# Squares of twelve weight blocks taken as products on TensorE instead of passes on ScalarE, with new booked lengths in the planner and one more block asked early

## The chip, the cores and the metric

The kernel runs on one core of a Trainium2 chip. The metric is the device time of one execution in microseconds (us). Engines are named as in the profile: PE is TensorE (its weight loads stand apart as PEld), DVE is VectorE, ACT is ScalarE, POOL is GpSimd, SP is SyncE, which only asks for DMA transfers here.

## The reference

Three layers follow each other: a two-sided attention, a feed-forward layer with squared ReLU, and a layer of eight experts of which each token uses one.

```python
def _attn_ref(x, state):            # x 8,8,512,64   state 8,8,32,64
    scores = scale * x @ state^T;  a = softmax(scores);   xread = a @ state
    scores2 = scale * state @ x^T; a2 = softmax(scores2); sread = a2 @ x
    return concatenate([xread, sread], axis=2)
def _moe_ref(x, w_in, w_out):       # 4608 x 512, 512 x 2048, 2048 x 512
    r = np.maximum(x @ w_in, 0.0)
    return (r * r) @ w_out
def _moe2_ref(x, expert_emb, tau, w1, w2):
    expert_idx = argmax(logits)     # logits: cosine of x and expert_emb, over tau
    out[mask] = gate_w * (np.maximum(x[mask] @ w1[e], 0.0) @ w2[e])
```

The two weights w_in and w_out come as float64; the rest is float32.

## The kernel before

PE multiplies in 16-bit halves: a float32 operand is scaled by a power of two and split into a high and a low half, and three products stand for one. The scale of each 256-column block of w_in comes from the largest sum of squares of its columns, the scale of w_out from the sum of all its squares. So every weight block passes ScalarE and VectorE several times before PE can use it, and this work fills the first 100 us.

The 8 MB of each float64 weight come in 16 blocks of 1 MB, in the order of `BLOCKS`: two blocks of w_in ("i"), two of w_out ("o"), and so on: blocks 0, 1, 4, 5, 8, 9, 12, 13 are w_in's i0 to i7, blocks 2, 3, 6, 7, 10, 11, 14, 15 w_out's o0 to o7. `weights()` asks for them one after the other on SP's queue; from block `AHEAD` on only after the two DMA transposes of the first attention (L553) are asked. For each block, `to_f32` (L900)
- converts the upper parts of the 1024 numbers on ACT into a "top", one of two tiles that alternate (rec_128 and rec_129 in the order rows; L915),
- widens the top into the block's float32 place, on ACT (L922) or DVE (L925), whichever has less booked,
- adds the lower bits on DVE (L928), and lets the scale be worked out: `wi_scale` (L941) squares a w_in block on ACT (L947), sums the squares down the columns with four PE products against a tile of ones (L955), takes the largest on DVE (L961); `wo_square` (L1000) squares and sums a w_out block in one ACT pass (L1006).

With the scale (swi) known, the state of the first attention times the block (L668) is split on ACT and DVE into sw (L677, L317), and the up-projection of the first 256 tokens (unit 0) can run on PE (L1395 to L1397); its ReLU is ACT L1348, its square ACT L1352, and its down-projection is done in float32 on PE (L1458), two weight blocks at a time. The weight blocks themselves are split on ACT (L993, L1054) and DVE (L317).

The order of the instructions on every engine is written by a planner (class `Plan`) when the program is built: threads yield an engine and a booked length (`act(n)`, `dve(n)`, `pe(k, n)`), and the one that can start first goes next, with a priority for ties. The booked lengths decide the order only; each engine then works its list strictly in that order. Further names: ps_t and ps_u are pools of two PSUM banks each (tiles "t" and "u"), `stage`, `he`, `g`, `wo_t` are places where raw blocks land, and rid is a small table (34.5 KB) asked behind block 9; SP's next request, of rec_d, waits for a POOL copy of it (L1872).

Of the kernel before, what the change touches and what calls it, by code (L numbers as in the profile page):

```python
# [10 lines left out]
F32 = mybir.dt.float32  # L11
# [38 lines left out]
LOADER = 9  # L50
AHEAD = 5
PRIO_A0 = 0.8
# [193 lines left out]
def moe_kernel(  # L246
# [79 lines left out]
    def splits(pieces, n):  # L326

        at, times = plan.now(), []
        for hi, lo, src, scale in pieces:
            yield act(n) + (at,)  # L330
            nc.scalar.activation(out=hi, in_=src, func=AF.Copy, scale=scale)
            times.append(plan.now())
        for (hi, lo, src, scale), t in zip(pieces, times):
            yield dve(n) + (t,)
            split_lo(lo, src, scale, hi)
# [115 lines left out]
    def attention(b):  # L451
# [8 lines left out]
        for i in range(2):  # L460
            q = slice(2 * i, 2 * i + 2)
            yield act(1024)
            nc.scalar.activation(out=xh.bitcast(BF16)[:, q], in_=xf[:, q], func=AF.Square, accum_out=ss[:, i:i + 1])
        yield act(256)
        nc.scalar.activation(out=xl.bitcast(BF16)[:, :, :64], in_=stt, func=AF.Square, accum_out=ss[:, 2:3])
# [98 lines left out]
    def first_attention():  # L564

        yield ev("st", 0)
        stt = st_t.pop(0)
        yield xhl_slots
        xh, xl = halves_tile()
        ss = small.tile([128, 3], F32, name="ss")  # L570
        yield act(256)
# [39 lines left out]
    def first_scale(ss, stt):  # L611
# [6 lines left out]
        for i in range(2):  # L618
            yield pjk_slots
            jk = att.tile([128, 2, 512], BF16, name="pjk")  # L620
            yield act(1024)
            nc.scalar.activation(out=jk, in_=xf[:, 2 * i:2 * i + 2], func=AF.Square, accum_out=ss[:, i:i + 1])
            pjk_slots.release()
# [126 lines left out]
    def state_side(b, pairs, scl):  # L750
# [21 lines left out]
        for C, p in enumerate(ps):  # L772
# [4 lines left out]
                            op1=ALU.mult)  # L777
            yield act(700)
            nc.scalar.activation(out=e2[:, C, :], in_=p, func=AF.Exp, scale=scl, bias=mt[:, C:C + 1],
# [115 lines left out]
    def to_f32(n, dst, squares, squared):  # L895
# [4 lines left out]
        if not W64:  # L900
            w = raw.bitcast(F32)
            plan.add(squares(w), plan.cur[1])
            for m in over:
# [3 lines left out]
        else:  # L907
# [5 lines left out]
            top = tops[k_t % 2]  # L913
            yield act(1024)
            nc.scalar.activation(out=top.bitcast(F16), in_=raw.bitcast(BF16)[:, :, 2], func=AF.Copy)  # L915
            at = plan.now()
            for m in over:
                yield ev("read", m)
            plan.cur[2] = max(at, plan.now())
# [12 lines left out]
        plan.add(freed(n, slots, squared), plan.cur[1])  # L932

    def freed(n, slots, squared):
# [5 lines left out]

    def wi_scale(q, w):  # L941
        at = plan.now()
        yield pjk_slots
        plan.cur[2] = max(at, plan.now())
        sq = att.tile([128, 4, BW], BF16, name="pjk")
        yield act(1024)
        nc.scalar.activation(out=sq, in_=w.rearrange("p (k f) -> p k f", k=4), func=AF.Square)  # L947
        ev("wisq", q).set()
# [3 lines left out]
        p, k_h = ps_u.tile([128, 512], F32, name="u"), u_slots.last()  # L952
        yield pe(4, BW)
# [10 lines left out]
        if q % 2:  # L964
# [5 lines left out]
            v = w  # L970
            V.tensor_scalar(out=v, in0=v, scalar1=FLOOR, scalar2=None, op0=ALU.max)
            pow2(swi[:, qs], iswi[:, qs], v, 204)
# [7 lines left out]
    def wi_block(n, q):  # L980
        yield ev("raw", n)
        yield from to_f32(n, wi32[q].rearrange("p k f -> p (k f)"), lambda a: wi_scale(q, a), ev("wisq", q))
        ev("wi32", q).set()
        plan.add(wi_split(q), PRIO_SPLIT)
# [14 lines left out]

    def wo_square(q, w):  # L1000
# [4 lines left out]
        yield act(1024)  # L1005
        nc.scalar.activation(out=jk, in_=w, func=AF.Square, accum_out=woacc[:, q:q + 1])  # L1006
        pjk_slots.release()
        ev("wosq", q).set()

    def wo_block(n, q):  # L1010
        yield ev("raw", n)
        yield from to_f32(n, wo32[q].rearrange("p k d -> p (k d)"), lambda a: wo_square(q, a), ev("wosq", q))
        ev("f32", q).set()

    def weights():
# [13 lines left out]
        V.tensor_reduce(out=ismin[:, 0:1], in_=iswi, axis=X, op=ALU.max)  # L1029
        yield from tensor_scale(woacc, smin[:, 1:2], ismin[:, 1:2])  # L1030
        yield tiny(3)
# [27 lines left out]

    def tensor_scale(acc, s, inv):  # L1060

# [10 lines left out]
        yield tiny(4)  # L1072
        V.tensor_scalar(out=w, in0=p[:, 0:1], scalar1=FLOOR, scalar2=None, op0=ALU.max)
        t_slots.release()
# [3 lines left out]
    def experts():  # L1078
# [46 lines left out]
        def scale():  # L1125
            for i in range(2 * NE):
# [3 lines left out]
                for n in range(2 * i, 2 * i + 2):  # L1130
                    yield ev("stage", n)
                    for a in range(2):
                        yield pjk_slots
                        jk = att.tile([128, 1024], BF16, name="pjk")
                        col = 2 * (n % 2) + a
                        yield act(1024)
                        nc.scalar.activation(out=jk, in_=halves[n].bitcast(F32)[:, a * 1024:a * 1024 + 1024],
# [73 lines left out]
    def route_tile(i, ps, k_h, rc, st):  # L1211
# [3 lines left out]
        if i < 2 * F32U:  # L1215
            yield ev("wo scale")
        yield act(600)
        nc.scalar.activation(out=rc[:, 0:512].bitcast(BF16), in_=ps, func=AF.Square, accum_out=st["f2"][:, j:j + 1],
# [719 lines left out]
```

## Time and profile before

| | us |
|---|---|
| three runs | 1081.05, 1079.14, 1084.92; median 1081.05 |
| profiled execution, its own time | 1085.53 |
| its span in the trace | 1083.7 |
| busy in the span: PE | 1034.8 (95%) |
| DVE | 669.9 (62%) |
| ACT | 600.3 (55%) |
| POOL | 122.9 (11%) |

The profiled execution takes 1.8 us more than its span and lies 0.4% above the median of the runs. Busy shares are means over stages: in the first 110 us the weights and the first attention are prepared, from there to about 610 us the rest of attention and the first two layers run, then the experts.

### The profile page before, as it was taken

How to read it: one execution, taken by the hardware profiler on the slowest of the kernel's cores; microseconds unless marked ns; L12 is line 12 of the kernel's file. 1: busy time of each engine (PE TensorE's matmuls, PEld its weight loads, DVE VectorE, ACT ScalarE, POOL GpSimd, SP SyncE). 2: the span in 40 equal slices, each digit the busy share in tenths (PEclk: the TensorE clock that was granted, in tenths of full speed). 3: DMA queues.
4: the chain of work that ended last, by engine and by line, in shares of the span. 5: the costliest groups of instructions: out<-in, count | busy, mean ns of one | idle time of the engine just before them, and what ended most of it. 6: DMA issues, size and time to landing. Idle time of an engine off the chain costs nothing. (4 is left out here: it accounts for less than half of the span.)

```text
span 1083.7 us, 26223 instructions
## 1 busy us (share of the span) xinstructions
PE 1034.8 (95%) x10553; PEld 667.1 (62%) x10553; DVE 669.9 (62%) x1818; ACT 600.3 (55%) x1003; POOL 122.9 (11%) x149
## 2 busy tenths in 40 slices
PE   5789999899999999999999999999999999999998
PEld 4345465455565555656565666677676766767674
DVE  6779888778798877788887873465222222322222
ACT  6999898878887878879888783211111110101010
POOL 0000002002001001020010010321112111112111
PEclk9999999999999999999999999999999999999999
DMA  8843566755836655756766778834895767684792
GB/s 272 321 172 106 143 200 159 247 164 171 237 116 167 212 139 183 214 137 204 211 210 219 252 212 295 224 81 137 309 237 159 212 173 216 198 249 150 168 295 87
DMA packets 161599, 212.91 MB, mean 196 GB/s; under 512 B 112257, under 2 KB 115201, under 8 KB 156098
## 3 DMA queue, kind: packets, MB, share of 16 engines
q1 hardware_dynamic: 152722, 184.04, 58.1%
q0 software_dynamic: 8320, 27.08, 7.7%
q8 instruction: 84, 1.38, 0.5%
q14 instruction: 41, 0.34, 0.1%
q10 hardware_dynamic: 432, 0.08, 0.0%
HBM read 259.10 MB, written 51.68 MB: 287 GB/s over the span
## 5 line engine op out<-in xcount | busy, mean ns | idle before, releaser
L1745 ACT ACTIVATE r<-u 128x512 f32<-128x512 f32 x70 | 41.8, 597 | 323.3 <-PE u L1791 294.0
L1481 PE MATMUL d<-wo_t,g 128*128 128x512 f16 x512 | 194.1, 379 | 1.8 <-DVE g L1367 1.7
L1479 PE MATMUL d<-wo_t,g 128*128 128x512 f16 x512 | 194.0, 379 | 1.5 <-DVE g L1365 0.6
L1480 PE MATMUL d<-wo_t,g 128*128 128x512 f16 x512 | 194.0, 379 | 0.0
L1395 PE MATMUL u<-aT,sw 128*128 128x256 f16 x512 | 141.1, 276 | 7.7 <-ACT sw L677 4.3
L1397 PE MATMUL u<-aT,sw 128*128 128x256 f16 x512 | 140.8, 275 | 1.3 <-DVE sw L317 0.7
L1396 PE MATMUL u<-aT,sw 128*128 128x256 f16 x512 | 140.9, 275 | 0.5 <-issue 0.4
L1748 DVE CAST hh<-r 128x512 f16<-128x512 f32 x70 | 30.0, 429 | 137.3 <-ACT r L1745 135.8
L1348 ACT ACTIVATE r<-u,cg 128x512 f32<-128x512 f32 x128 | 87.5, 683 | 46.8 <-PE u L1397 22.8
L1759 DVE TENSOR_SCALAR o<-d,rec,wo_t 128x512 f32<-128x512 f32 x35 | 28.3, 809 | 107.6 <-PE d L1814 107.5
L1367 DVE TENSOR_TENSOR g<-r,g 128x512 f16<-128x512 f32 x128 | 87.7, 687 | 9.8 <-ACT r L1362 7.8
L1321 POOL DMA_INDIRECT rec_d<-rec,pi x34 | 37.6, 1105 | 494.0 <-DVE mt L774 91.2
L1814 PEld LDWEIGHTS <-hh 128*128 128x128 f16 (+1 forms) x688 | 54.6, 102 | 57.1 <-issue 0.4
L1481 PEld LDWEIGHTS <-g 128*128 128x128 f16 x512 | 50.0, 98 | 63.6 <-DVE g L1367 3.7
L1362 ACT ACTIVATE r<-r 128x512 f32<-128x512 f32 x128 | 80.2, 628 | 1.5
L1479 PEld LDWEIGHTS <-g 128*128 128x128 f16 x512 | 50.3, 98 | 49.2 <-DVE g L1365 1.1
L1480 PEld LDWEIGHTS <-g 128*128 128x128 f16 x512 | 50.1, 98 | 47.7 <-issue 0.9
L1789 PE MATMUL u<-xes,stage 128*128 128x128 f16 x448 | 76.1, 219 | 0.4 <-issue 0.4
L1790 PE MATMUL u<-xes,stage 128*128 128x128 f16 x448 | 76.1, 219 | 0.0
L1791 PE MATMUL u<-xes,stage 128*128 128x128 f16 x448 | 76.1, 219 | 0.0
L1395 PEld LDWEIGHTS <-sw 128*128 128x128 f16 x512 | 51.4, 100 | 33.0 <-issue 16.7
L1789 PE MATMUL u<-xes,xx 128*128 128x128 f16 x416 | 70.5, 219 | 0.0
(331 smaller groups left out, 2564.8 us busy)
## 6 DMA issues: line engine op xcount, KB each, us to landing
w_d<-he SPq DMA_DIRECT2D x128, 256.0 KB
g<-w_d SPq DMA_DIRECT2D x16, 2048.0 KB
wo_t<-w_d SPq DMA_DIRECT2D x16, 2048.0 KB
stage<-w_d SPq DMA_DIRECT2D x14, 2048.0 KB
he<-w_d SPq DMA_DIRECT2D x14, 2048.0 KB
xx<-w_d SPq DMA_DIRECT2D x13, 2048.0 KB
sw<-w_d SPq DMA_DIRECT2D x13, 2048.0 KB
stage<-in_w_dram SPq DMA_DIRECT2D x20, 1024.0 KB
```

The source lines that it names most:

```text
L1348: nc.scalar.activation(out=r, in_=ps, func=AF.Relu, scale=cg[:, g:g + 1] if u >= F32U else cgq[:, c:c + 1])
L1362: nc.scalar.activation(out=r, in_=r, func=AF.Square)
L1367: V.tensor_tensor(out=gl, in0=r, in1=gh, op=ALU.subtract)
L1395: mm(o, lhsT=hl[:, i, 0, fs], rhs=aT[:, i, :], start=i == 0, stop=False)
L1396: mm(o, lhsT=hl[:, i, 0, fs], rhs=aT[:, 2 + i, :], start=False, stop=False)
L1397: mm(o, lhsT=hl[:, i, 1, fs], rhs=aT[:, i, :], start=False, stop=i == 1)
L1479: mm(ps, lhsT=g_h[:, f, ts], rhs=w[:, 0, :], start=f == 0, stop=False)
L1480: mm(ps, lhsT=g_h[:, f, ts], rhs=w[:, 1, :], start=False, stop=False)
L1481: mm(ps, lhsT=g_l[:, f, ts], rhs=w[:, 0, :], start=False, stop=f == KF - 1)
L1789: mm(p[:, j, xs], lhsT=w[:, 0, k, fs], rhs=xe[:, k, xs], start=k == 0, stop=False)
L1790: mm(p[:, j, xs], lhsT=w[:, 0, k, fs], rhs=xe[:, 4 + k, xs], start=False, stop=False)
L1791: mm(p[:, j, xs], lhsT=w[:, 1, k, fs], rhs=xe[:, k, xs], start=False, stop=k == 3)
```

## The change

For blocks 4 to 15 (`GRAM`) the squares are no longer passes on ACT. Eight PE products of the block's top with itself (128 by 128 each, every one with its own weights) are summed in a bank of ps_t; the diagonal holds the sums of squares. For w_in a DVE multiplication with the identity (128 x 256) leaves the diagonal, and one PE product with the ones in place of four spreads the sums; for w_out DVE multiplies (128 x 128) and sums (128 x 128). Since the tops lack the lower bits, the sums get a margin of 1.14 and 1.13. A top is now free again only when its products are done. The planner's `act(...)` bookings change: passes with a sum are booked at 1260 instead of 1024, the strided conversion at 1130, splits 100 longer, and so on; this alters no instruction, only the order. `AHEAD` is 6 instead of 5. The bookings and the new threads also move instructions on all engines.

```diff
-AHEAD = 5
+AHEAD = 6
+GRAM = tuple(range(4, 16))
@@ splits
-            yield act(n) + (at,)
+            yield act(n + 100) + (at,)
@@ attention (and alike at the other passes with a sum)
-            yield act(1024)
+            yield act(1260)
@@ to_f32
-            yield act(1024)
+            yield act(1130)
             nc.scalar.activation(out=top.bitcast(F16), in_=raw.bitcast(BF16)[:, :, 2], func=AF.Copy)
+            gram = n in GRAM
+            if gram:
+                plan.add(squares(top, True), plan.cur[1])
...
-            top_slots.release(k_t)
...
-            plan.add(squares(dst), plan.cur[1])
+            if gram:
+                plan.add(topped(k_t, squared), plan.cur[1])
+            else:
+                top_slots.release(k_t)
+                plan.add(squares(dst, False), plan.cur[1])
@@ wi_scale
+        if gram:
+            yield t_slots
+            p = ps_t.tile([128, 512], F32, name="t")[:, 0:BW].rearrange("p (c m) -> p c m", c=2)
+            yield pe(8, 140)
+            for c in range(2):
+                for k in range(4):
+                    mm(p[:, c], lhsT=w[:, k, c], rhs=w[:, k, c], start=k == 0, stop=k == 3)
+            ev("wisum", q).set()
...
+            yield dve(BW)
+            V.tensor_tensor(out=sq.rearrange("p k (c m) -> p (k c) m", c=2), in0=p,
+                            in1=ident16.unsqueeze(1).to_broadcast([128, 2, 128]), op=ALU.mult)
+            t_slots.release()
...
-        for k in range(4):
-            mm(p[:, 0:BW], lhsT=oneb, rhs=sq[:, k, :], start=k == 0, stop=k == 3)
+        for k in range(ks):
+            mm(p[:, 0:BW], lhsT=oneb, rhs=sq[:, k, :], start=k == 0, stop=k == ks - 1)
@@ wo_square
+        if gram:
+            yield t_slots
+            p = ps_t.tile([128, 512], F32, name="t")[:, 0:128]
+            yield pe(8, 140)
+            for c in range(8):
+                mm(p, lhsT=w[:, 128 * c:128 * c + 128], rhs=w[:, 128 * c:128 * c + 128], start=c == 0, stop=c == 7)
+            yield dve(128)
+            V.tensor_tensor(out=p, in0=p, in1=ident16, op=ALU.mult)
+            yield dve(128)
+            V.tensor_reduce(out=woacc[:, q:q + 1], in_=p, axis=X, op=ALU.add)
```

Three places in the order of the instructions matter below. The first is PE just ahead of the first up-projection. Before, the last products with the ones for i1 (L955) stand there, and the up-projection follows:

```order
L955 LDWEIGHTS oneb
L955 MATMUL u<-pjk,oneb 128x256
L1395 LDWEIGHTS sw
L1395 MATMUL u<-aT,sw 128x256
L1396 LDWEIGHTS sw
L1396 MATMUL u<-aT,sw 128x256
```

In the changed kernel the same place (L962 are products of tops, L1442 and L1443 the up-projection) reads:

```order
L962 LDWEIGHTS rec_129
L962 MATMUL t<-rec_129 128x128
L1442 LDWEIGHTS sw
L1442 MATMUL u<-aT,sw 128x256
L1443 LDWEIGHTS sw
L1443 MATMUL u<-aT,sw 128x256
```

Sixteen products, eight of block 4 (rec_128) and eight of block 5 (rec_129), now stand between the ones of i1 and the first up-projection.

The second place is ACT from the first split of sw on. Before (L677 sw, L993 split of a w_in block, L1348 and L1352 ReLU and square of unit 0):

```order
L677 ACTIVATE sw<-S_250,swi 128x512
L993 ACTIVATE wi<-wi,swi 128x1024
L677 ACTIVATE sw<-S_251,swi 128x512
L915 ACTIVATE rec_129<-g 128x1024
L922 CAST wi<-rec_129 128x1024
L947 ACTIVATE pjk<-wi 128x1024
L915 ACTIVATE rec_128<-he 128x1024
L1348 ACTIVATE r<-u,cgq 128x512
L947 ACTIVATE pjk<-wi 128x1024
L1352 ACTIVATE g<-r 128x2x2x128
L922 CAST wo_t<-rec_128 128x1024
```

In the changed kernel (L678 sw, L1023 split, L916 conversion, L926 widening, L1052 square of a w_out block, L1395 and L1399 ReLU and square):

```order
L678 ACTIVATE sw<-S_248,swi 128x512
L1023 ACTIVATE wi<-wi,swi 128x1024
L678 ACTIVATE sw<-S_249,swi 128x512
L916 ACTIVATE rec_129<-g 128x1024
L916 ACTIVATE rec_128<-he 128x1024
L926 CAST wi<-rec_129 128x1024
L1052 ACTIVATE pjk,woacc<-wo_t 128x1024
L1395 ACTIVATE r<-u,cgq 128x512
L926 CAST wo_t<-rec_128 128x1024
L1399 ACTIVATE g<-r 128x2x2x128
L916 ACTIVATE rec_129<-wo_t 128x1024
L1023 ACTIVATE wi<-wi,swi 128x1024
```

The two squares L947 have left this stretch, a square of a w_out block that stood ahead of it has come in, and conversions of later blocks have moved up.

The third place is SP's queue at the start. Before (L339 is every plain load, L553 the transposes):

```order
L339 DMA stage<-in_w_out_dram 128x2x2048 x2
L339 DMA g<-in_w_in_dram 128x4x1024
L553 DMA_TRANSPOSE aT<-xx 128x8x128 x2
L339 DMA g<-in_w_in_dram 128x4x1024
L339 DMA he<-in_w_out_dram 128x2x2048
L339 DMA wo_t<-in_w_out_dram 128x2x2048
```

In the changed kernel:

```order
L340 DMA stage<-in_w_out_dram 128x2x2048 x2
L340 DMA g<-in_w_in_dram 128x4x1024 x2
L554 DMA_TRANSPOSE aT<-xx 128x8x128 x2
L340 DMA he<-in_w_out_dram 128x2x2048
L340 DMA wo_t<-in_w_out_dram 128x2x2048
```

Block 5 (the second g) has moved ahead of the two transposes; the order of the requests behind it, down to the tables, rec_d, block 10 and the second x, is as before.

## Rows read from the trace of the kernel before

**Rows 1.** Windows by stage: length, busy time of each engine, granted PE clock, DMA share, GB/s

```profile
27.00:54.00 27.00, 21.13 (x141) 10.46 (x142) 21.06 (x44) 24.40 (x33) 2.20 (x5) 0.96 0.85 321
54.00:81.00 27.00, 24.07 (x123) 12.66 (x124) 19.76 (x49) 25.31 (x38) 1.42 (x2) 0.91 0.47 170
```

**Rows 2.** Timeline of PE: start, length, what [idle before, released by]

```profile
28.96 0.40 PE L1395 MATMUL u<-aT,sw 128*128 128x256 f16 x1 [3.85 <-ACT sw L677]
...
36.43 0.42 PE L1396 MATMUL u<-aT,sw 128*128 128x256 f16 x1
36.64 0.42 PE L1397 MATMUL u<-aT,sw 128*128 128x256 f16 x1
...
39.08 0.27 PE L1397 MATMUL u<-aT,sw 128*128 128x256 f16 x1
39.19 7.03 PE L1458 MATMUL d<-wo_t,g 128*128 128x512 f32 x16
...
51.38 0.61 PE L955 MATMUL u<-pjk,oneb 128*128 128x256 bf16 x4 [2.54 <-ACT r L1348]
...
64.00 0.39 PE L471 MATMUL t<-ss,one 128*128 128x3 f32 x2 [1.92 <-ACT xx L465]
...
65.52 1.01 PE L955 MATMUL u<-pjk,oneb 128*128 128x256 bf16 x4 [1.01 <-ACT pjk L947]
...
91.48 3.60 PE L1458 MATMUL d<-wo_t,g 128*128 128x512 f32 x8
```

**Rows 3.** Windows of 2 us, columns as in rows 1

```profile
52.00:54.00 2.00, 2.00 (x33) 0.78 (x34) 1.98 (x3) 2.00 (x4) 0.00 (x0) 0.50 1.01 406
54.00:56.00 2.00, 2.00 (x4) 0.94 (x5) 0.78 (x1) 2.00 (x5) 0.00 (x0) 0.69 1.05 387
...
66.00:68.00 2.00, 2.00 (x11) 1.37 (x10) 1.74 (x10) 2.00 (x3) 0.00 (x0) 0.50 0.65 264
68.00:70.00 2.00, 2.00 (x26) 1.01 (x24) 1.53 (x2) 1.36 (x3) 0.00 (x0) 0.78 0.00 0
```

**Rows 4.** Timeline of ACT, columns as in rows 2

```profile
30.41 1.12 ACT L915 ACTIVATE rec<-g 128x1024 f16<-128x1024 bf16 x1
31.57 1.04 ACT L922 CAST wi<-rec 128x1024 f32<-128x1024 bf16 x1
32.52 1.05 ACT L947 ACTIVATE pjk<-wi 128x1024 bf16<-128x1024 f32 x1
33.48 1.10 ACT L915 ACTIVATE rec<-he 128x1024 f16<-128x1024 bf16 x1
34.48 0.67 ACT L1348 ACTIVATE r<-u,cgq 128x512 f32<-128x512 f32 x1
...
43.69 1.06 ACT L1006 ACTIVATE pjk<-wo_t 128x1024 bf16<-128x1024 f32 x1
...
44.73 1.16 ACT L915 ACTIVATE rec<-stage 128x1024 f16<-128x1024 bf16 x1
...
48.69 1.12 ACT L915 ACTIVATE rec<-he 128x1024 f16<-128x1024 bf16 x1 [1.75 <-DMA he<-in_w_out_dram]
```

**Rows 5.** Timelines of SP and POOL and windows: block 9, tables, block 10

```profile
43.52 0.41 SPq L339 DMA_DIRECT2D he<-in_w_out_dram  x1
...
41.88 1.19 POOL L1872 COPY rec<-rid 128x1 int32<-128x1 int32 x1 [40.10 <-DMA rid<-in_rowid_dram]
...
22.00:24.00 2.00, 1.11 (x16) 0.33 (x17) 2.00 (x4) 2.00 (x4) 0.00 (x0) 1.00 0.02 4
```

**Rows 6.** Prices: a DVE pass over 256 numbers in PSUM, two 128-column products

```profile
38.73 0.42 DVE L961 TENSOR_REDUCE wv<-u 128x1 f32<-128x256 f32 x1 [2.24 <-PE u L955]
...
700.05 0.22 PE L1789 MATMUL u<-xes,xx 128*128 128x128 f16 x1
700.10 0.22 PE L1790 MATMUL u<-xes,xx 128*128 128x128 f16 x1
```

**Rows 7.** PE's waits from 100 us to the end: us in total, times, longest

```profile
PE t L471 <- ACT xx L465: 3.0, 4, 1.2
```

More of the change, by code (lines that the diff above doesn't have):

```diff
@@ L461, in attention @@
             q = slice(2 * i, 2 * i + 2)
-            yield act(1024)
+            yield act(1260)
             nc.scalar.activation(out=xh.bitcast(BF16)[:, q], in_=xf[:, q], func=AF.Square, accum_out=ss[:, i:i + 1])
-        yield act(256)
+        yield act(490)
         nc.scalar.activation(out=xl.bitcast(BF16)[:, :, :64], in_=stt, func=AF.Square, accum_out=ss[:, 2:3])
@@ L570, in first_attention @@
         ss = small.tile([128, 3], F32, name="ss")
-        yield act(256)
+        yield act(490)
         nc.scalar.activation(out=xl.bitcast(BF16)[:, :, :64], in_=stt, func=AF.Square, accum_out=ss[:, 2:3])
@@ L620, in first_scale @@
             jk = att.tile([128, 2, 512], BF16, name="pjk")
-            yield act(1024)
+            yield act(1260)
             nc.scalar.activation(out=jk, in_=xf[:, 2 * i:2 * i + 2], func=AF.Square, accum_out=ss[:, i:i + 1])
@@ L777, in state_side @@
                             op1=ALU.mult)
-            yield act(700)
+            yield act(920)
             nc.scalar.activation(out=e2[:, C, :], in_=p, func=AF.Exp, scale=scl, bias=mt[:, C:C + 1],
@@ L901, in to_f32 @@
             w = raw.bitcast(F32)
-            plan.add(squares(w), plan.cur[1])
+            plan.add(squares(w, False), plan.cur[1])
             for m in over:
@@ L913, in to_f32 @@
             top = tops[k_t % 2]
-            yield act(1024)
+            yield act(1130)
             nc.scalar.activation(out=top.bitcast(F16), in_=raw.bitcast(BF16)[:, :, 2], func=AF.Copy)
-            at = plan.now()
+            converted = plan.now()
+            gram = n in GRAM
+            if gram:
+                plan.add(squares(top, True), plan.cur[1])
             for m in over:
                 yield ev("read", m)
-            plan.cur[2] = max(at, plan.now())
+            plan.cur[2] = max(converted, plan.now())
             if plan.load("act") < plan.load("dve"):
@@ L929, in to_f32, with topped @@
                                    op0=ALU.logical_shift_right, op1=ALU.bitwise_or)
-            plan.add(squares(dst), plan.cur[1])
+            if gram:
[3 more added lines that the diff above has]
+                plan.add(squares(dst, False), plan.cur[1])
             squared = ev("raw", n)
         plan.add(freed(n, slots, squared), plan.cur[1])
+    def topped(k_t, squared):
+        yield squared
+        top_slots.release(k_t)
     def freed(n, slots, squared):
@@ L939, in moe_kernel, with wi_scale @@
     wv = {}
-    def wi_scale(q, w):
+    def wi_scale(q, w, gram):
+        if gram:
+            at = plan.now()
+            yield t_slots
+            plan.cur[2] = max(at, plan.now())
+            p = ps_t.tile([128, 512], F32, name="t")[:, 0:BW].rearrange("p (c m) -> p c m", c=2)
+            w = w.rearrange("p (k c m) -> p k c m", k=4, c=2)
+            yield pe(8, 140)
[3 more added lines that the diff above has]
+            ev("wisum", q).set()
         at = plan.now()
@@ L944, in wi_scale @@
         plan.cur[2] = max(at, plan.now())
-        sq = att.tile([128, 4, BW], BF16, name="pjk")
-        yield act(1024)
-        nc.scalar.activation(out=sq, in_=w.rearrange("p (k f) -> p k f", k=4), func=AF.Square)
+        ks = 1 if gram else 4
+        sq = att.tile([128, 4, BW], BF16, name="pjk")[:, :ks]
+        if gram:
[3 more added lines that the diff above has]
+            t_slots.release()
+        else:
+            yield act(1024)
+            nc.scalar.activation(out=sq, in_=w.rearrange("p (k f) -> p k f", k=4), func=AF.Square)
+            ev("wisum", q).set()
         ev("wisq", q).set()
@@ L952, in wi_scale @@
         p, k_h = ps_u.tile([128, 512], F32, name="u"), u_slots.last()
-        yield pe(4, BW)
-        for k in range(4):
-            mm(p[:, 0:BW], lhsT=oneb, rhs=sq[:, k, :], start=k == 0, stop=k == 3)
+        yield pe(ks, BW)
+        for k in range(ks):
+            mm(p[:, 0:BW], lhsT=oneb, rhs=sq[:, k, :], start=k == 0, stop=k == ks - 1)
         pjk_slots.release()
@@ L970, in wi_scale @@
             v = w
-            V.tensor_scalar(out=v, in0=v, scalar1=FLOOR, scalar2=None, op0=ALU.max)
+            V.tensor_scalar(out=v, in0=v, scalar1=1.14, scalar2=FLOOR, op0=ALU.mult, op1=ALU.max)
             pow2(swi[:, qs], iswi[:, qs], v, 204)
@@ L981, in wi_block @@
         yield ev("raw", n)
-        yield from to_f32(n, wi32[q].rearrange("p k f -> p (k f)"), lambda a: wi_scale(q, a), ev("wisq", q))
+        yield from to_f32(n, wi32[q].rearrange("p k f -> p (k f)"), lambda *a: wi_scale(q, *a), ev("wisum", q))
         ev("wi32", q).set()
@@ L998, in moe_kernel, with wo_square @@
     woacc = small.tile([128, NB], F32, name="woacc", bufs=1)
-    def wo_square(q, w):
+    def wo_square(q, w, gram):
+        if gram:
+            at = plan.now()
+            yield t_slots
+            plan.cur[2] = max(at, plan.now())
+            p = ps_t.tile([128, 512], F32, name="t")[:, 0:128]
+            yield pe(8, 140)
+            for c in range(8):
+                mm(p, lhsT=w[:, 128 * c:128 * c + 128], rhs=w[:, 128 * c:128 * c + 128], start=c == 0, stop=c == 7)
+            ev("wosum", q).set()
+            yield dve(128)
+            V.tensor_tensor(out=p, in0=p, in1=ident16, op=ALU.mult)
+            yield dve(128)
+            V.tensor_reduce(out=woacc[:, q:q + 1], in_=p, axis=X, op=ALU.add)
+            t_slots.release()
+            ev("wosq", q).set()
+            return
         at = plan.now()
@@ L1004, in wo_square @@
         jk = att.tile([128, 1024], BF16, name="pjk")
-        yield act(1024)
+        yield act(1260)
         nc.scalar.activation(out=jk, in_=w, func=AF.Square, accum_out=woacc[:, q:q + 1])
         pjk_slots.release()
+        ev("wosum", q).set()
         ev("wosq", q).set()
@@ L1011, in wo_block @@
         yield ev("raw", n)
-        yield from to_f32(n, wo32[q].rearrange("p k d -> p (k d)"), lambda a: wo_square(q, a), ev("wosq", q))
+        yield from to_f32(n, wo32[q].rearrange("p k d -> p (k d)"), lambda *a: wo_square(q, *a), ev("wosum", q))
         ev("f32", q).set()
@@ L1029, in weights @@
         V.tensor_reduce(out=ismin[:, 0:1], in_=iswi, axis=X, op=ALU.max)
-        yield from tensor_scale(woacc, smin[:, 1:2], ismin[:, 1:2])
+        yield from tensor_scale(woacc, smin[:, 1:2], ismin[:, 1:2], 1.13)
         yield tiny(3)
@@ L1058, in wo_split, with tensor_scale @@
         ev("wo", q).set()
-    def tensor_scale(acc, s, inv):
+    def tensor_scale(acc, s, inv, margin=1.0):
         v = small.tile([128, 1], F32, name="fv")
@@ L1072, in tensor_scale @@
         yield tiny(4)
-        V.tensor_scalar(out=w, in0=p[:, 0:1], scalar1=FLOOR, scalar2=None, op0=ALU.max)
+        V.tensor_scalar(out=w, in0=p[:, 0:1], scalar1=margin, scalar2=FLOOR, op0=ALU.mult, op1=ALU.max)
         t_slots.release()
@@ L1135, in scale @@
                         col = 2 * (n % 2) + a
-                        yield act(1024)
+                        yield act(1260)
                         nc.scalar.activation(out=jk, in_=halves[n].bitcast(F32)[:, a * 1024:a * 1024 + 1024],
@@ L1216, in route_tile @@
             yield ev("wo scale")
-        yield act(600)
+        yield act(740)
         nc.scalar.activation(out=rc[:, 0:512].bitcast(BF16), in_=ps, func=AF.Square, accum_out=st["f2"][:, j:j + 1],
```

## The prediction

> **What bounds the kernel now.** I read the windows by stage first, then PE's timeline, then that of ACT, and last the queues. PE is busy for 1034.8 of 1083.7 us, so outside the first 100 us the time is almost wholly PE's own work, which the change leaves alone apart from its products of tops. What can be won are PE's waits and its slow stretches. In the windows of 27 to 54 and 54 to 81 us [rows 1] PE stands still for 5.9 and 2.9 us, while ACT is busy for 24.4 and 25.3 of 27: ACT is what the start hangs on. PE's timeline [rows 2] names the waits behind the first up-projection: 2.54 us until 51.38 (a bank of ps_u that ACT's ReLU frees late), 1.92 until 64.00 (the attention's squares on ACT) and 1.01 until 65.52 (a weight block's square on ACT): 5.5 us.
>
> Two of these waits are followed by a stretch at the lower clock. The granted clock is 0.50 and 0.69 in the two windows from 52 and 0.50 and 0.78 in the two from 66 [rows 3]; with 2.4 GHz as 1.00, PE lost 1.0 + 0.6 + 1.0 + 0.4 = 3.1 us of full speed there. (At the start the spacing of 256-column products says the same: 0.21 us at 36.43, the level of 1.2 GHz, 0.11 us at 39.08, that of 2.4 GHz [rows 2].) So between 39.19, when the float32 down-projection of unit 0 begins, and its end at 91.48 + 3.60 = 95.08 [rows 2], 5.5 + 3.1 = **8.6 us** are not work.
>
> **The change, part by part.** *ACT.* Six squares L947 go, at 0.96 us from start to start (32.52 to 33.48), and six L1006, at 1.04 (43.69 to 44.73) [rows 4]: 12.0 us. By the order three more widenings (10 in place of 7) stand on ACT at 0.95 each (31.57 to 32.52): 2.9 back, so ACT has 9.1 us less to do before the weights are ready. That covers the 8.6, if the time comes out at the places where PE waits. It does by the order: the attention's squares come nine places earlier in ACT's list and its x is late only by the load (below), and no pass of a weight block stands between a product of tops and its sum.
>
> *DVE.* Six multiplications over 256 numbers in PSUM at about the 0.42 of L961 [rows 6], six pairs over 128 at no more than that each, less three widenings: some 3 to 5 us more. DVE is busy for 21.1 and 19.8 of 27 us [rows 1], so its idle time hides it; without that cover it would come on top.
>
> *PE.* 96 products of 128 columns at 0.055 us (two of them start 700.05 and 700.10, at a neighbouring spacing of 0.05 to 0.06, each with a weight load of its own [rows 6]) and 18 fewer products with the ones at 0.11. For blocks 8 to 15, which fall behind the start of the down-projection, that is 64 x 0.055 - 12 x 0.11 = **+2.2 us**, all on the path, since PE sets the end there.
>
> *The first up-projection.* It now stands behind the products of block 5, which need that block's conversion. The passes ahead of this conversion (sw, a split, sw) are the same, so it runs from 30.4 to 31.4 as now [rows 4], and eight products at the lower clock (twice 0.055) end at 32.3: 3.3 us later than 28.96. But the first ReLU comes no later: behind that conversion ACT has a conversion (1.00), a widening (0.95) and a square (1.04), and reaches the ReLU at 34.4, against 34.48 now [rows 4]. So PE's delay meets ACT's own pace. The start of the down-projection then slips by something between nothing and the whole 3.3; 16 products at the lower clock (1.8) less six with the ones (1.3) are 0.5 more work until there, and I take **+1.1**, nearer the lower end, because the ReLUs set the pace.
>
> *The early block.* The DMA engines stand idle from 22 to 24 us (share 0.02 [rows 5]), between the loads asked before the transposes and those after. With block 5 asked ahead, its 1 MB (2.6 us at the 390 to 405 GB/s of the windows from 52 [rows 3]) fills the gap. Blocks 6 to 9 are still asked behind the transposes; these come about 2 us later, because in ACT's order the copy that they turn now stands behind the square of i1. Four blocks then take 10.5 us from about 27, and the table rid, asked behind them, lands near 39.9, against 41.88 now, when POOL's copy starts [rows 5]. Block 10 waits for that copy and would be asked at 41.5 in place of 43.52 [rows 5]; now its conversion starts at 48.69 [rows 4], and x, one load behind, is there 2.6 us later, at 51.3: it would land near 49.3. These 2 us matter, since ACT now stands ready for x at about 47, directly behind block 10's conversion; now ACT waits 1.75 us for block 10 [rows 4]. The Trainium skill (DMA: Bandwidth & Descriptors, Queues, rings and completion order) says that each DMA engine consumes the descriptors of a queue in the order of its ring. By that rule rid moves up with the bulk ahead of it and the sum is the one taken here; were rid's landing tied to nothing ahead of it, the first rival's would hold. The trace agrees so far: five loads of 2.6 us from about 25 end near 39, and the copy that waits for rid starts at 41.88 [rows 5].
>
> From x at 49.3 ACT has, by its order, twenty passes to the fifth square of unit 0; between the 0.67 of a ReLU and the 1.12 of a conversion [rows 4], and each 0.1 shorter from start to start, I take 0.8 as their mean: 65.3. PE comes to the fifth down-projection from 40.3 with four of them (14.2, from 7.03 and 3.60 [rows 2]), 48 products of the up-projection (5.3), 56 of tops (3.1) and some 3 us of small work, at about 65.9. ACT is ahead of PE by about half a microsecond: enough, but no more. So the waits of 2.54, 1.92 and 1.01 should go, and with them the slow stretches.
>
> *The bookings.* They change no pass, only where PE's list has the product that follows the attention's squares (L471). The old booking was 2 x 0.95 + 0.31 = 2.26 us by the formula of `act`, the measured passes take about 2.5, the new booking is 2.80. Behind 100 us PE waits 3.0 us in four places for these squares [rows 7]. Four times 0.54 is the most that this can give back, 2.2; nothing is the least, and a worse order elsewhere could cost as much; I take **1.0**.
>
> **Sum:** -8.6 + 2.2 + 1.1 - 1.0 = -6.3 us. Against the profiled execution's own 1085.53 (span 1083.7 and 1.8 around it) that is 1079.2. The runs' median is 4.5 us lower, and a saving in the start is as large there: 1081.05 - 6.3 = **1075** us.
>
> **The rivals.** *The waits come back elsewhere.* For it: ACT's lead on PE is some 0.6 us, and x is a load that no engine can hasten. If rid lands no earlier, x comes at 51.3, the third pair of the down-projection slips by 2 us, and a wait of that size was followed by 1.4 to 1.6 us at the lower clock in both places [rows 3]. Of the 6.3 then 2.7 stay: 1078. Against it: the gap in the DMA's work at 22 us is plain and block 5 fits into it.
>
> *Slower.* PE works its list strictly in order, and the sixteen products of blocks 8 and 9 stand ahead of the third chunk's up-projection. If block 9's conversion on ACT comes d later than PE wants it, PE waits d, the chunk's ReLU comes later, and the slow stretch follows (1.6). If the old waits also remain because ACT is filled by its widenings, the time is 2.2 + 1.1 + 1.6 + d above now, which passes 5.4 from d = 0.5 on; with d = 2 it is 1088. Against it: that conversion stands twelve passes of about 0.8 behind the first ReLU at 34.4, so near 45, and PE, busy with 7.03 us of float32 work [rows 2] from 40.3, asks for it at 47.3.
>
> *More.* The lead holds, the bookings give their 2.2 and the down-projection starts no later: -8.6 + 2.2 - 2.2 = -8.6, or 1072.5.
>
> **How the numbers follow.** About 0.5% (5.4 us) is what a measurement of this kernel can tell from no change. The forecast has 0.58, with a range of its own from 1072.5 to 1079 (the 3.3 and the two bounds of the bookings); 0.42 of it lies beyond 5.4 and 0.16 within. The waits that come back have 0.25 (within), more has 0.10 (faster), slower 0.07. That makes faster 0.52, within 0.5% 0.41, slower 0.07. The range from 1070 to 1082 takes in the first three and leaves out the slower case and the far ends.
>
> **What would show it.** Right: the last float32 down-projection of unit 0 ends near 90 instead of 95; the first up-projection starts near 32.3 and the first ReLU still near 34.4; no wait of PE over 1 us and no window below 0.9 of the clock between 42 and 90; ACT busy about 9 us less in all; POOL's copy of rid starts near 40. Wrong: waits of PE for a conversion (ACT rec) ahead of products of tops, or for x's squares near 50; a clock of 0.50 in a window behind 42; a down-projection that starts behind 42; or a start that is 6 us shorter with as much more idle time of PE between 110 and 650, where the order is new as well.

## The result: 0.7% slower

The changed kernel takes 1088.54 us (median of 8 runs, 1086.62 to 1093.91), the kernel before 1081.09 (8 runs): ratio 1.0072, 95% interval 1.005 to 1.0094. The forecast was 1075, and its range ended at 1082. The profiled execution took 1086.81 us (span 1084.9). ACT is busy for 591.3 us in place of 600.3, PE for 1034.9 in place of 1034.8.

The start went much as forecast. Windows by stage of the changed kernel, columns as in [rows 1]:

```profile
27.00:54.00 27.00, 22.00 (x189) 13.72 (x190) 23.08 (x50) 23.79 (x30) 1.36 (x5) 1.00 0.85 309
54.00:81.00 27.00, 26.31 (x181) 14.91 (x180) 24.81 (x61) 24.83 (x34) 0.61 (x2) 1.00 0.43 158
```

PE's timeline of the changed kernel, as in [rows 2]:

```profile
27.68 1.04 PE L962 MATMUL t<-rec 128*128 128x128 bf16 x8 [3.67 <-ACT rec L916]
31.97 1.03 PE L962 MATMUL t<-rec 128*128 128x128 bf16 x8 [3.25 <-ACT rec L916]
...
87.43 3.60 PE L1505 MATMUL d<-wo_t,g 128*128 128x512 f32 x8
```

From 54 to 81 us PE now stands still for 0.7 us in place of 2.9, and the clock is 1.00 in place of 0.91. The last float32 down-projection of unit 0 ends at 91.03 in place of 95.08 [rows 2]. The products of tops wait 3.67 and 3.25 us for their conversions, ahead of the first up-projection. So there is a lead of 4 us at 91, and a loss of 7 at the end. Where it goes is best seen in a second pair of traces, taken when both kernels ran once more (medians 1078.87 and 1072.82 us; below). The two are of different chips, on which the kernel before takes 1072.70 and 1072.61 us. In them, PE's busy time in three windows and then 676 to 700, of the changed kernel:

```profile
100.00:300.00 200.00, 195.24 (x1768) 114.42 (x1768) 164.96 (x432) 166.76 (x291) 10.98 (x16) 1.00 0.62 171
300.00:500.00 200.00, 198.44 (x1744) 117.81 (x1742) 165.70 (x463) 168.28 (x294) 18.95 (x24) 1.00 0.68 186
500.00:676.00 176.00, 174.41 (x1323) 107.90 (x1320) 130.53 (x410) 131.72 (x217) 20.32 (x24) 1.00 0.75 230
676.00:700.00 24.00, 15.01 (x164) 12.72 (x163) 3.55 (x10) 2.57 (x5) 2.00 (x3) 0.82 1.09 214
```

and the same windows of the kernel before:

```profile
100.00:300.00 200.00, 192.21 (x1711) 113.11 (x1710) 162.51 (x422) 168.91 (x296) 12.38 (x16) 1.00 0.65 185
300.00:500.00 200.00, 196.89 (x1755) 116.47 (x1754) 164.23 (x466) 165.52 (x291) 17.35 (x24) 1.00 0.59 167
500.00:676.00 176.00, 173.72 (x1336) 108.28 (x1335) 131.51 (x389) 132.82 (x216) 10.19 (x15) 1.00 0.75 231
676.00:700.00 24.00, 23.27 (x247) 15.68 (x245) 11.17 (x48) 5.86 (x11) 10.32 (x11) 1.00 0.94 234
```

Up to 676 the new order is even the denser one: 568.1 us of PE work against 562.8, 5.3 more. Then PE does 15.01 us of work in 24, at a mean clock of 0.82, where the kernel before does 23.27 at 1.00. PE's timeline there, first the kernel before (its last float16 down-projection), then the changed kernel:

```profile
689.76 0.38 PE L1481 MATMUL d<-wo_t,g 128*128 128x512 f16 x1
```

```profile
679.27 0.38 PE L1528 MATMUL d<-wo_t,g 128*128 128x512 f16 x1
686.30 0.27 PE L1836 MATMUL u<-xes,stage 128*128 128x128 f16 x1 [6.64 <-DMA xes<-rec]
...
696.66 0.22 PE L1836 MATMUL u<-xes,xx 128*128 128x128 f16 x1 [2.34 <-DMA xes<-rec]
...
1048.82 0.20 PE L1836 MATMUL u<-xes,g 128*128 128x64 f16 x1 [2.69 <-issue]
```

```profile
686.00:690.00 4.00, 3.70 (x36) 3.73 (x37) 0.00 (x0) 0.00 (x0) 0.00 (x0) 0.50 1.11 309
```

The changed kernel reaches the end of the second layer 10.5 us sooner (679.27 against 689.76; the layer ends near 690, not at the 610 that the section on the profile gives). Then it waits 6.64 and 2.34 us for xes, the transposed tokens of the first two expert tiles, and behind the first wait it works at a granted clock of 0.50 until about 691 (the last row). It loses the lead and 5 us more. Over 676 to 700, 8.3 us of this are more idle time of PE. The later wait of 2.69 (behind nothing that the profile names) is hardly part of it, because the kernel before has one of 2.1 too. The first pair of traces shows waits of 5.89 and 1.50 us for xes at the same place.

Why xes is late stands on SP's queue. The changed kernel: stores of the experts' split weights (w_d), three loads of 2 MB each (L1742), the first transposed load (L1782):

```profile
653.54 1.00 SPq L340 DMA_DIRECT2D w_d<-he  x2
656.86 0.37 SPq L1742 DMA_DIRECT2D stage<-w_d  x1
658.91 0.34 SPq L1742 DMA_DIRECT2D he<-w_d  x1
660.76 0.34 SPq L1742 DMA_DIRECT2D xx<-w_d  x1
673.40 1.36 SPq L1782 DMA_TRANSPOSE xes<-rec  x1
```

The kernel before, in the other trace of this pair:

```profile
647.30 3.85 SPq L339 DMA_DIRECT2D w_d<-he  x4
653.31 0.36 SPq L1695 DMA_DIRECT2D stage<-w_d  x1
655.36 0.34 SPq L1695 DMA_DIRECT2D he<-w_d  x1
663.64 0.35 SPq L1695 DMA_DIRECT2D xx<-w_d  x1
679.87 1.25 SPq L1735 DMA_TRANSPOSE xes<-rec  x1
```

In the kernel before, the three loads are asked 37, 35 and 26 us ahead of the end of the second layer (690.14); in the changed kernel 23, 21 and 19 us (679.65). They wait for the experts' chain, in which ACT and DVE scale and split eight experts' weights that go to memory and come back. By the new order its last store is asked 3.4 us later (654.54 against 651.15), although PE is 10.5 us ahead. The first transposed load of the changed kernel is asked at 673.40, and its tokens reach PE at 686.30, 12.9 us later. Of that, 3.9 us pass until its first packet moves, at 677.3, and the last packet of the three loads ends at 678.3. The other 9.0 us the transposed load itself is under way. Windows of the changed kernel:

```profile
671.00:676.00 5.00, 5.00 (x25) 2.25 (x23) 1.90 (x10) 0.36 (x1) 2.99 (x3) 1.00 0.97 393
676.00:681.00 5.00, 3.65 (x17) 1.47 (x15) 0.47 (x4) 0.69 (x2) 2.00 (x3) 1.00 1.17 189
```

The DMA engines move 393 GB/s until 676. Over the next 5 us they are as busy (share 1.17) but move 189: POOL's gathers and the transposes, xes among them, now run at the same time in small packets. No run takes these two apart.

### The profile page after: what moved, and what is told of

Read it like the earlier page. It is cut to its first block, busy times and chain, and to the rows that moved or that the text cites. A ratio compares the mean times of both kernels' runs of the same rounds, so it can differ in the third digit from the quotient of the medians.

```text
span 1084.9 us, 26367 instructions
## 1 busy us (share of the span) xinstructions
PE 1034.9 (95%) x10631; PEld 673.0 (62%) x10631; DVE 671.9 (62%) x1835; ACT 591.3 (54%) x986; POOL 123.4 (11%) x149
## 5 line engine op out<-in xcount | busy, mean ns | idle before, releaser
L1442 PE MATMUL u<-aT,sw 128*128 128x256 f16 x512 | 140.5, 274 | 4.3 <-ACT r L1395 3.5
L1443 PE MATMUL u<-aT,sw 128*128 128x256 f16 x512 | 140.2, 274 | 0.0
L1395 ACT ACTIVATE r<-u,cg 128x512 f32<-128x512 f32 x128 | 87.3, 683 | 54.8 <-PE u L1444 40.9
L1836 PE MATMUL u<-xes,stage 128*128 128x128 f16 x448 | 77.8, 222 | 5.9 <-DMA xes<-rec 5.9
L1837 PE MATMUL u<-xes,stage 128*128 128x128 f16 x448 | 77.8, 222 | 0.0
L1838 PE MATMUL u<-xes,stage 128*128 128x128 f16 x448 | 77.7, 222 | 0.0
L1836 PE MATMUL u<-xes,xx 128*128 128x128 f16 x416 | 70.5, 219 | 1.5 <-DMA xes<-rec 1.5
L1838 PE MATMUL u<-xes,xx 128*128 128x128 f16 x416 | 70.4, 219 | 0.0
```

Of the source, the lines that this page charges most:

```text
L1395: nc.scalar.activation(out=r, in_=ps, func=AF.Relu, scale=cg[:, g:g + 1] if u >= F32U else cgq[:, c:c + 1])
L1442: mm(o, lhsT=hl[:, i, 0, fs], rhs=aT[:, i, :], start=i == 0, stop=False)
L1443: mm(o, lhsT=hl[:, i, 0, fs], rhs=aT[:, 2 + i, :], start=False, stop=False)
L1836: mm(p[:, j, xs], lhsT=w[:, 0, k, fs], rhs=xe[:, k, xs], start=k == 0, stop=False)
L1837: mm(p[:, j, xs], lhsT=w[:, 0, k, fs], rhs=xe[:, 4 + k, xs], start=False, stop=False)
L1838: mm(p[:, j, xs], lhsT=w[:, 1, k, fs], rhs=xe[:, k, xs], start=False, stop=k == 3)
```

## The experiments

They ran on three chips, on each of which the kernel before takes 1072 to 1073 us (1081 in the first result); each ratio is to runs of the kernel before on the same chip. The first four texts use these theories: A, PE's lead is lost at the change to the experts, because the first xes stands behind late loads; B, the gather or the weights themselves are late; C, the products of tops cost the time.

**The order of two requests.** The third load is held until the first xes is asked (after and, as a control, before):

```diff
                         yield ev("moe1") if name == "w2" else ev("cum", NXT - 1)
+                        if name == "w1":
+                            yield ev("xe", 0)
```

> The changed kernel, with the load of the second expert tile's first weight (2 MB into xx) asked only behind the first turned tile (xes) instead of ahead of it; up to 660 us its order is the same. Theory A (the start is shorter, but PE comes to the experts 9 us earlier and stands there, because the first xes queues behind 2 MB that were asked late): the wait of 5.9 us at 685 and the slow clock behind it go, the time falls by 6 to 9 us against the changed kernel, to a ratio of 0.997 to 1.001 against the kernel before. Rival B (PE waits there for the gather or the weights themselves): the wait stays within 1.5 us of 5.9 and the ratio near 1.007. Rival C (the products or the early part cost the time): no change, 1.007.

Measured 1.0001 (0.9982 to 1.002): as A expected, outside B and C. SP's queue and PE's timeline of this run:

```profile
660.07 0.37 SPq L1744 DMA_DIRECT2D stage<-w_d  x1
662.13 0.34 SPq L1744 DMA_DIRECT2D he<-w_d  x1
675.07 1.27 SPq L1784 DMA_TRANSPOSE xes<-rec  x1
...
682.42 0.35 SPq L1744 DMA_DIRECT2D xx<-w_d  x1
```

```profile
679.30 0.22 PE L1838 MATMUL u<-xes,stage 128*128 128x128 f16 x1 [1.70 <-DMA xes<-rec]
...
692.30 0.22 PE L1838 MATMUL u<-xes,xx 128*128 128x128 f16 x1 [2.09 <-DMA xx<-w_d]
```

With one load fewer ahead of it, xes reaches PE 4.2 us after it is asked, not 12.9. The held load is now itself late (2.09 at 692.30), so part of the gain goes back. The Trainium skill (DMA: Bandwidth & Descriptors, Queues, rings and completion order) says that each DMA engine takes the descriptors of a queue in the order of its ring. By that rule a small transfer waits for the bulk ahead of it, and the trace agrees in part: with the third load held, the first packet of xes moves 2.2 us after its request (677.3) in place of 3.9. The larger part of the 8.7 us is behind that: from its first packet to PE it takes 2.0 us in place of 9.0, now that most of the gathers are through before it.

> The same edit in the kernel before, as a control. A: PE does not wait for xes there, so within 2 us of the kernel before (0.998 to 1.002). If the edit itself is good or bad for another reason, it shows here too.

Measured 1.0041 (1.0022 to 1.006), outside what A expected: in the kernel before the same two lines make PE wait 2.3 us for the held load. So they are no gain in themselves; they help only where xes is in the way.

**The bookings alone.** The changed kernel with the old `act(...)` numbers, and the kernel before with the new ones:

```diff
-            yield act(1260)
+            yield act(1024)
...
-            yield act(n + 100) + (at,)
+            yield act(n) + (at,)
```

> The changed kernel with the old bookings of ACT's passes: products of tops and the early block alone. In its order the first xes stands ahead of the 2 MB load by itself. A: the start ends about 4 us earlier than in the kernel before, no wait above 2 us at the start of the experts, ratio 0.992 to 0.998. C (the products cost the time): 1.005 or more.

Measured 1.0101 (1.0075 to 1.0127). PE's waits in the old-bookings run:

```profile
96.96 0.27 PE L1442 MATMUL u<-aT,sw 128*128 128x256 f16 x1 [2.64 <-ACT r L1395]
...
261.10 1.01 PE L768 MATMUL t<-xx,sthl 128*64 128x512 f16 x6 [2.29 <-DVE lg L1294]
```

> The kernel before with the new bookings alone: squares on ACT, five early blocks. A: the start is as long as before or 1 to 2 us shorter, the 2 MB load stands ahead of the first xes, PE is less far ahead and waits 0 to 3 us: ratio 0.999 to 1.004. If the bookings alone are what costs: 1.006 or more. If they help by themselves: under 0.997.

Measured 1.008 (1.0062 to 1.0097), and the first xes keeps PE waiting here too:

```profile
695.12 0.27 PE L1789 MATMUL u<-xes,stage 128*128 128x128 f16 x1 [5.74 <-DMA xes<-rec]
```

A missed both, and the first number lies where C expected it, so C was still open. The bookings alone cost as much as the whole change, and taking them out does not give it back. Contrary to what stands above of the bookings, they do not change the order only. The planner also gives the widening of a top, and a rounding of the squared ReLU, to ACT or DVE by what each has booked: in the kernel before with the new bookings ACT has 991 instructions and DVE 1830, in place of 1003 and 1818, so 12 passes moved. What is common to these slow kernels is that the planner made the order anew. This led to the next theory A: the start is better, the order behind it worse.

**Start and order apart.** Here the planner goes by its own rules until it has booked 95 us; from there it takes the steps in the order written down from the other kernel (`PLANNED`, a table of thread names; a second table gives the roundings the same engine as there):

```diff
+                    rank = RANK.get((th[4], th[5])) if self.follow else None
+                    if rank is not None and (known is None or rank < known[0]):
+                        known = (rank, key, th, dep)
...
+                self.follow = self.follow or start >= FOLLOW
```

> The changed kernel, with its own start; from the point where the plan has booked 95 us the work goes in the order that the kernel before had (the rows of every engine's queue are those of before from there on). Nothing is left out. Theory A (the lead of the start is real; the time goes where the rest of the program is put in another order, above all at the first transposed load of the experts): the lead of some 4 us at 95 us is kept, no wait over 2 us for the first transposed load, ratio to before 0.993 to 0.998. Theory C (the products or the earlier start cost the time themselves): 1.004 or more, as the changed kernel. Theory D (no lead of the start reaches the end, in whatever order): 0.999 to 1.002.

Measured 0.9975 (0.9957 to 0.9994): as A expected, and far from C; the upper end of the interval touches the 0.999 of D.

> The reverse: the kernel before, with its own start and its squares on ScalarE, and from 95 us of the plan on the order of the changed kernel. Nothing is left out. Theory A: 1.004 to 1.012, the wait for the first transposed load of the experts is there again, shorter by the 4 us that this start is later (1 to 3 us). Theory C: 0.998 to 1.002. Theory D: what the changed kernel has, 1.005 to 1.009.

Measured 1.01 (1.0072 to 1.0129): as A, with an interval that also takes in the upper end of D. From its timeline, the wait expected to be shorter is not:

```profile
695.81 0.27 PE L1870 MATMUL u<-xes,stage 128*128 128x128 f16 x1 [6.24 <-DMA xes<-rec]
```

> The changed kernel itself, unchanged, on the chip of these three runs, so that traces and ratios of one chip stand beside each other. All theories: ratio 1.005 to 1.0094 as measured first, a wait of 5 to 7 us for the first transposed load of the experts.

Measured 1.0052 (1.0032 to 1.0072); its rows are those of the section above. With the order of before, the start of the changed kernel is worth 0.25%; the order of the changed kernel, behind the start of before, costs 1%.

**The experts' chain earlier.**

```diff
-PRIO_E1 = 2.2
+PRIO_E1 = 1.4
```

> The changed kernel with one number changed, the rank of the experts' scaling and splitting after the attention (PRIO_E1 2.2 to 1.4), so that their stores end earlier; the second tile's weight is still asked for ahead of the first transposed load. Theory A: stores end some 8 us earlier, the loads of 2 MB with them, the wait for the first transposed load falls from 5.89 us to under 2, ratio 0.999 to 1.003. Theory B (that load waits for its gather or for the routing, not for the loads ahead of it): the wait stays over 4 us, ratio 1.005 to 1.009.

Measured 0.9982 (0.9965 to 0.9998), somewhat better than A expected and outside B. Last stores, loads and xes of this run:

```profile
641.49 2.54 SPq L340 DMA_DIRECT2D w_d<-he  x4
646.23 0.36 SPq L1742 DMA_DIRECT2D stage<-w_d  x1
...
659.05 0.35 SPq L1742 DMA_DIRECT2D xx<-w_d  x1
673.31 1.25 SPq L1782 DMA_TRANSPOSE xes<-rec  x1
```

xes is asked at the same time as in the changed kernel (673.31 against 673.40), the first two loads 10.6 us earlier; PE has no wait for xes left. One priority takes back 0.7%.

**What shortens the start.** Sixth block and products apart, with the order of before behind:

```diff
-AHEAD = 5
+AHEAD = 6
```

> The kernel before with one part of the change, the sixth raw block asked for ahead of the second half of the first states (AHEAD 5 to 6); squares on ScalarE and bookings as before, and from 95 us of the plan on the order of the kernel before. Nothing is left out. Theory S (the start is shorter because twelve squares leave ScalarE's queue): the waits of 2.54, 1.92 and 1.01 us for squares and sums stay, the last fp32 down-projection of unit 0 stays within 1 us of its time before, ratio 0.999 to 1.003. Theory L (it is shorter because its blocks come earlier): it ends 2 us or more earlier, ratio 0.995 to 0.998.

Measured 0.9979 (0.9967 to 0.9992): as L expected.

> The changed kernel with that one part taken out (AHEAD 6 to 5): products of the tops and the new bookings in the start, the order of the kernel before from 70 us of the plan on. Nothing is left out. Theory S: the waits of 2.54 and 1.92 us for squares are gone, and the half speed of the clock with them; the last fp32 down-projection of unit 0 ends 2 to 4 us earlier than before, ratio 0.996 to 0.999. Theory L: it ends within 1 us of before, ratio 0.999 to 1.004.

Measured 1.0015 (1.0 to 1.003): the ratio of L, not that of S. This run has the products and, up to 70 us, also the new bookings; where it is called the run of the products, both are meant.

> The kernel before itself, unchanged, as one more kernel of this call: its ratio to its own other runs is what the measurement tells from no change, and its trace stands beside the two others of one chip. All theories: 0.998 to 1.002, two stretches at half clock between 50 and 70 us, no wait over 1 us for the first transposed load of the experts.

Measured 1.0001 (0.9989 to 1.0012). The last float32 down-projection of unit 0 in the kernel before, with the sixth block alone, with the products and five early blocks, and with both (the changed start with the order of before):

```profile
89.71 3.60 PE L1458 MATMUL d<-wo_t,g 128*128 128x512 f32 x8
```

```profile
86.51 3.60 PE L1538 MATMUL d<-wo_t,g 128*128 128x512 f32 x8
```

```profile
91.09 3.60 PE L1585 MATMUL d<-wo_t,g 128*128 128x512 f32 x8
```

```profile
87.08 3.60 PE L1585 MATMUL d<-wo_t,g 128*128 128x512 f32 x8
```

These ends (start and length added) are 93.31, 90.11, 94.69 and 90.68. Counted from the first product on x, which starts when x has landed (6.55, 7.03, 7.19 and 6.65), they are 86.8, 83.1, 87.5 and 84.0, with one trace for each. So the sixth block brings 3.7 us without the products and 3.5 with them, and the products cost 0.7 and 1.0. Theory S was wrong in the sum: with all its squares on ACT, the run with the sixth block has waits of 1.62 and 1.68 us behind 40 in place of 2.48, 1.94 and 1.01, and the clock is 1.00 in the window from 54 to 81 (0.94 before).

In one part S was right. In the run of the products no wait behind 40 is above 0.94 us. But the float32 down-projection begins later there, because PE waits for the conversion of block 5 ahead of the first up-projection. Its first rows in the kernel before, with the sixth block, with the products (with that wait ahead of them), and with both:

```profile
38.05 7.03 PE L1458 MATMUL d<-wo_t,g 128*128 128x512 f32 x16
```

```profile
37.29 3.60 PE L1538 MATMUL d<-wo_t,g 128*128 128x512 f32 x8
```

```profile
33.17 1.03 PE L1040 MATMUL t<-rec 128*128 128x128 bf16 x8 [4.34 <-ACT rec L994]
...
40.60 3.60 PE L1585 MATMUL d<-wo_t,g 128*128 128x512 f32 x8
```

```profile
39.92 7.09 PE L1585 MATMUL d<-wo_t,g 128*128 128x512 f32 x16
```

The products put the start of the down-projection back by 2.6 us, with the sixth block and without it (by 3.0 and 1.9 counted from x), and take the waits behind it away; the two nearly cancel. In the run of the products the clock over 54 to 81 is still 0.94.

What the block does is seen in the DMA view of 14 to 50 us, in 40 slices of 0.9 us, in the kernel before:

```profile
DMA  9999999930299799999999999999400083999999
```

and with the sixth block asked early:

```profile
DMA  9999999999999999999999999800009499999999
```

The hole near 22 us is filled, and what follows is asked earlier: the table rid by 2.6 us, the next block by 2.0 and x by 1.5 (rec_d<-rec at 39.98 in place of 41.97). ACT had been waiting for blocks: in the window from 27 to 54 it is busy for 27.00 us in place of 25.23.

**The sixth block alone, and the rest left to the planner.** The kernel before with the same one number and no table:

> The kernel before with one number changed, AHEAD 5 to 6, and nothing held: the plan now puts the whole rest in an order of its own. Nothing is left out. The start is that of the run with the sixth block and the held order, so its last fp32 down-projection of unit 0 ends about 3 us earlier than before. Theory A (the order behind the start decides): the experts' stores end later than in the kernel before and the first transposed load waits 2 us or more, ratio 1.002 to 1.009, in spite of the same lead. Theory P (an order made anew is on the mean as good as the old one, and the sixth block's lead reaches the end): 0.996 to 0.999, as with the held order.

Measured 1.0051 (1.0031 to 1.0071). The total is as A expected, and the last store of the experts is asked 13.6 us later than in the kernel before (664.77 against 651.15). The place is not as expected: PE waits only 1.3 us for xes. It waits longer between 210 and 290, and behind two of the waits the mean clock is 0.60 (264 to 268) and 0.57 (285 to 289):

```profile
215.09 0.19 PE L807 MATMUL t<-he,xx 128*128 128x64 f16 x1 [2.65 <-DMA he<-he]
...
263.60 0.26 PE L1242 MATMUL t<-en,xr 128*128 128x16 f16 x4 [2.47 <-DMA xr<-rec]
...
284.04 0.39 PE L471 MATMUL t<-ss,one 128*128 128x3 f32 x2 [2.85 <-ACT xx L465]
```

## Why the prediction was wrong

- **The bookings** are the step that failed for the total: "They change no pass ... I take 1.0", with 2.2 as the most in either direction. The bound came from one group of waits [rows 7], as if the rest of the list stayed. That group did shrink as hoped, from 3.0 us to 0.6. But the new order behind 95 us measured +1.0% (some 11 us) behind the old start, the bookings alone +0.8%, and with them 12 passes changed their engine.
- **"A saving in the start is as large there"**, that is, at the end: it is only if what comes next is ready. In the changed kernel PE's lead even grew, to 10.5 us, and met loads that were asked no earlier. With the order of before a lead of 2.6 us at 91 (90.68 against 93.31) arrived: 0.9975 is 2.7 us less at the end.
- **The start's size** was near: a lead of 4.1 us in the first pair of traces and 2.9 in the second (90.43 against 93.31), instead of 5.3 (8.6 less 2.2 and 1.1). PE waits no longer than 1.0 us between 40 and 100, the clock is 1.00 from 27 to 100, and ACT has 9.0 us less to do in all (forecast 9.1).
- **The start's cause** was wrong in the main. "ACT is what the start hangs on" took an engine that was itself waiting for loads for the bound. The waits of 2.54, 1.92 and 1.01 us shrink with all squares left on ACT, once the sixth block fills the hole in the loads; the prediction priced that block as the cover for the squares' gain, but it was the net gain. The products do take the waits away, as forecast, and give as much back ahead of the down-projection.
- **The +1.1 for the first up-projection** came out by luck. The down-projection begins at 40.20 in place of 39.19 (forecast 40.3). In the later traces it begins 1.9 us later (39.92 against 38.05), and this is the sum of 0.8 us that the sixth block brings forward and 2.6 that the products put back. PE's waits for conversions ahead of products of tops (3.67 and 3.25 us) were a mark for "wrong". The ReLUs did not set the pace either: the first came at 36.49, not 34.4, behind a wait of 0.81 us for PE.
- **The early block's 2 us for rid and x** came to 0.6 and about 1: POOL's copy started at 41.29 (forecast 39.9, before 41.88), and ACT began with x at 50.40 (forecast 49.3), behind a wait of 1.26. The forecast's own numbers say as much, since four loads of 2.6 us from 27 end only half a microsecond ahead of five from 25. So x came almost as late as in the rival of the waits that come back, and they did not come back.
- The last of the marks for "wrong" (a shorter start and as much more idle time behind 110) was the right suspicion, with too small a chance for a slower kernel (0.07, and by another way), and too early a place: up to 676 there was less idle time, not more.

Shown: that the order behind the start carries the loss, that in the changed kernel the change to the experts is its main place, that the sixth block makes the start's lead.

Open is why an order that the planner makes anew comes out 0.5 to 1.0% slower in four cases here (the changed kernel, the old bookings in it, the new ones alone, the sixth block alone), while a fifth, with one priority changed, is faster than before. Open is also the wait of 1.2 to 3.4 us between 943 and 960 or between 1038 and 1058 for which no releaser is seen; it stands in all traces but the first of the kernel before. In each of them a packet of 16 KB of the instruction queue lands 1.3 to 1.6 us before this wait ends (at 1047.44 for the wait until 1048.82), so PE may be waiting for its own instructions; that is not shown. The products were not tried without the sixth block in an order of the planner's own, nor with the old bookings in the held order, so what they cost in the start includes what the new bookings do there. Their run follows the table from 70 us, not 95.

Three versions are faster than both kernels by an interval that excludes 1: the start of the changed kernel with the order of before (0.9975), the kernel before with the sixth block and its old order (0.9979, and without the products), and the changed kernel with the experts' chain earlier (0.9982). They cannot be told apart.

## What to carry to other kernels

Where a planner writes the order, a change of costs or threads is a change of the whole program: measure it with the old order held behind the place that was changed, or the small local gain and the large accidental loss cannot be told apart. A lead on the busiest engine is worth only as much as the readiness of the next stage: look which transfers and which side chain that stage waits for, and what stands ahead of them on the queue. An engine busy for 25 of 27 us may still be waiting for data in turn; here a hole in the DMA row beside it was the cheaper thing to fill.

## What was not expected of the hardware

The same transposed load took 4.2 us from its request to its first use behind two loads of 2 MB, and 12.9 with a third, asked 1.9 us after the second; of these, 2.0 and 9.0 us lie behind its first packet, when the big loads were through or nearly so. Behind the wait of 6.64 us PE worked at half clock until about 691 (0.50 over 686 to 690), which cost another 2.3 us (an estimate: half of the stretch from 686.30 to 691). In the run of the sixth block with an order of its own the clock fell behind the waits of 2.47 and 2.85 us too, and behind 2.65 it did not (1.00 over 215 to 219).
